# Two loads moved forward and one group of operands split in the front of a convolution and token-mixing kernel

## The chip, the cores and the metric

The kernel runs on one core of a Trainium2 chip. The metric is the device time of one execution in microseconds (us), median over several runs. A ratio is the mean time of the fast runs of one kernel over that of the kernel before in the same rounds, so it is not quite the ratio of the medians that are quoted beside it. The kernel before was timed anew with each group of experiments, since each group ran on another chip (its medians there: 1449.39, 1450.40 and 1449.05 us).

## The reference, cut to what matters

```python
# x: 8 x 4224 x 192 (batch, tokens, channels); 8 heads of 24 channels; 7 taps
w = softmax(weight)                                  # 8 x 7
x = causal 7-tap convolution of x along the tokens, taps w by head
theta = x @ w_theta                                  # 192 x 192
zr, zi = x * cos(theta), x * sin(theta)
y = einsum('ts,bsd->btd', w_tok_r, zr) + einsum('ts,bsd->btd', w_tok_i, zi)   # 4224 x 4224 weights
u = x + y
out = u + maximum(u @ w_ch, 0)
```

## The kernel before

The 4224 tokens are 33 chunks of 128. For each chunk the kernel convolves (`conv`, two halves), transposes the result (`transpose`), multiplies by w_theta (`theta`, two halves), takes sine and cosine on ScalarE, and forms products and sums on VectorE. These become the moving operands of the large product. The weights of that product are loaded in **steps**, turned and combined on VectorE (`w_tasks`: the names "11", "21", "22", "12" are turned blocks, S1 to S4 sums of them), and used by the matmuls of line 443. In the **front**, the first 105 us or so, both kinds of work have to start together: chunks 0 to 10 are made while the first steps already run on those that are ready.

```python
    def banks(name, dtype=F32):              # PSUM buffer of conv, theta and transposes: two of them
        return mmpool.tile([P, 2, PC if dtype == F32 else 2 * PC], dtype, name=name, tag="mm")
    ...
        def w_tasks(self):                   # operands of a step, with their place in the step before
            ...
            return [
                (0.25, lambda: self.turn("11")), (1.2, lambda: self.turn("21")),
                (2.05, lambda: self.wsum("S3")), (2.2, lambda: self.turn("22")),
                (3.05, lambda: self.wsum("S1")), (3.3, lambda: self.wsum("S2")),
                (4.2, lambda: self.turn("12")), (5.1, lambda: self.wsum("S4")),
            ]
    ...
    load_chunk(0)
    ...
    load_chunk(1)
    ...
    steps[0].load_rows()
    for m in (1, 2):
        steps[0].load_w(m)                   # GpSimd queue; two buffers st, one per m
    load_chunk(2)                            # GpSimd queue
    for m in (1, 2):
        steps[1].load_w(m)                   # each waits until step 0 has turned that buffer
    for i in range(NW + 2):                  # NW = 11 chunks
        ...                                  # conv(0), theta(0) of i-1, conv(1), theta(1) of i-1
        if i == 1:
            for _, f in steps[0].w_tasks():
                f()
        if i + 3 < NW:
            load_chunk(i + 3)
        between(1)
        if ch:
            ch.transpose()
        if old:
            old.product(Z11)
        between(2)                           # matmuls of the steps, where ready
        if old:
            old.product(Z21)
        between(1)
        ...                                  # sums(0), sums(1)
```

The order of calls is the order on each compute engine.

Of the kernel before, what the change touches and what calls it, by code (L numbers as in the profile page):

```python
# [16 lines left out]
def kernel(  # L17
# [257 lines left out]
    def load_chunk(k):  # L275
        if k < NK and k not in chunks:
            chunks[k] = Chunk(k, before=chunks[k - 1] if k % NW else None)
# [229 lines left out]
    steps = [Step(t) for t in range(NSTEP)]  # L507
# [72 lines left out]
    def idle(n):  # L580
        for _ in range(n):
            pe(nc.tensor.matmul(
                spare[:, 0, 0:BH], lhsT=noise[:, 0:P], rhs=noise, start=True, stop=True
            ))
# [55 lines left out]
    def more(n):  # L640

        for i in range(n):
            if need[0] is None:
                need[0] = next(flow, NK)
            if need[0] > ready[0]:
                return n - i
            need[0] = next(flow, NK)
        return 0

    steps[0].load_rows()  # L650
    for m in (1, 2):
        steps[0].load_w(m)
    load_chunk(2)
    for m in (1, 2):
        steps[1].load_w(m)
    for i in range(NW + 2):
        ch = chunks.get(i) if i < NW else None
        old = chunks[i - 1] if 0 < i <= NW else None

        def between(n):  # L660
            left = more(n)
            if 0 < i < 3:
                idle(min(left, 2))

        if ch:
            ch.conv(0)
        between(2)
        if old:
            old.theta(0)
        between(1)  # L670
        if ch:
            ch.conv(1)
        if i == 0:
            idle(4)
        ready[0] = i - 2
        between(2)
        if old:
            old.theta(1)
        if i == 1:
            for _, f in steps[0].w_tasks():  # L680
                f()
        if i + 3 < NW:
            load_chunk(i + 3)
        between(1)
        if ch:
            ch.transpose()
        if old:
            old.product(Z11)
        between(2)
        if old:  # L690
            old.product(Z21)
        between(1)
        if old:
            old.sums(0)
        between(1)
        if old:
            old.sums(1)
        between(1)
# [37 lines left out]
```

## Time and profile before

| | before |
|---|---|
| time, median of 3 runs | 1449.51 us (1448.77 to 1449.61) |
| span of the profiled run | 1446.4 us |
| TensorE busy | 1416.3 us, 98% |
| TensorE's wait for x of chunk 3 | 0.88 us, at 26.8 to 27.7 us |

The page's rows of granted TensorE clock and of DMA, in 40 slices of the span (36 us each), are these:

```profile
PEclk9999999999999999999999999999999999999999
DMA  9986756465699998998899989999999999998893
```

In the first three slices, the front, the transfer engines are 80 to 90% busy or more, so the order of transfers counts there. The clock row reads 9 (90% or more) throughout, and hides stretches of a few microseconds at half clock. The lines that the argument rests on are in the prediction.

### The profile page before, as it was taken

What the parts mean: (1) busy time and instruction counts of PE and PEld (TensorE: products, weight loads), DVE (VectorE), ACT (ScalarE), POOL (GpSimd) and SP (SyncE); (2) the same over time, 40 slices, a digit from 0 to 9 for tenths busy, and PEclk for the clock granted to TensorE, in tenths of its full rate; (3) what the DMA queues carried; (4) which work ended last, traced back from release to release, by engine and by line L of the source; (5) the groups of instructions that cost most, each with busy time, mean ns of one, the idle gap of its engine ahead of it and who ended that gap; (6) DMA issues with size and microseconds to landing.
All of it is one profiled execution on the core that took longest, in us unless ns stands there. A gap on an engine that the chain in (4) does not pass through costs nothing.

```text
span 1446.4 us, 23748 instructions
## 1 busy us (share of the span) xinstructions
PE 1416.3 (98%) x9809; PEld 887.9 (61%) x9809; DVE 979.2 (68%) x1051; ACT 315.5 (22%) x379; POOL 435.1 (30%) x655
## 2 busy tenths in 40 slices
PE   7899999999999999999999999999999999999997
PEld 5556666666666666666666666666666666666665
DVE  6893555545548777866666657877777667767686
ACT  5861101111134254000000004435210110010133
POOL 7431211111233232432433342233323123213120
PEclk9999999999999999999999999999999999999999
DMA  9986756465699998998899989999999999998893
GB/s 173 227 178 145 146 103 149 90 149 97 137 231 219 214 250 217 228 254 183 213 256 213 242 143 245 228 188 234 279 216 206 209 204 221 204 203 194 166 222 125
DMA packets 272029, 281.99 MB, mean 195 GB/s; under 512 B 106672, under 2 KB 240176, under 8 KB 271920
## 3 DMA queue, kind: packets, MB, share of 16 engines
q0 software_dynamic: 162464, 92.15, 48.4%
q1 hardware_dynamic: 71824, 178.88, 35.1%
q10 hardware_dynamic: 37632, 9.44, 4.1%
q8 instruction: 77, 1.26, 0.3%
q14 instruction: 32, 0.26, 0.1%
HBM read 245.49 MB, written 108.13 MB: 244 GB/s over the span
## 4 chain that ended last, share of the span: by engine, by line
PE 89%; DVE 4%; DMA 3%; POOL 2%; ACT 1%; issue 1%; SPq 0%; DVEq 0%; ACTq 0%; POOLq 0%
PE y L443 82%; PE v L141 5%; PE pc L210 1%; PE tp L165 1%; POOL st L323 1%; DMA xw<-in_x_dram 1%; DVE z L257 1%; DVE wt L336 1%; DVE pv L408 1%; ACT z L246 1%; DVE z L251 0%; DVE pv L476 0%; DVE wt L348 0%; POOL xw L197 0%; DMA xs<-z 0%
## 5 line engine op out<-in xcount | busy, mean ns | idle before, releaser
L443 PE MATMUL y<-z,wt 128*128 128x384 f16 x7656 | 1283.6, 326 | 10.6 <-DVE pv L408 7.5
L443 PEld LDWEIGHTS <-wt 128*128 128x128 f16 x7656 | 740.8, 98 | 488.6 <-issue 10.6
L408 DVE TENSOR_TENSOR pv<-y,pv 128x768 f32<-128x768 f32 x324 | 308.9, 954 | 323.6 <-PE y L443 282.8
L336 DVE STREAM_TRANSPOSE wt<-st 128x1408 f16<-128x1408 f16 (+7 forms) x224 | 327.8, 1465 | 48.5 <-PE y L443 39.0
L323 POOL DMA_DIRECT2D st<-in_moe_w_tok_r_dram x232 | 132.5, 578 | 466.1 <-DVE wt L336 461.0
L323 POOL DMA_DIRECT2D st<-in_moe_w_tok_i_dram x232 | 132.7, 578 | 404.4 <-DVE wt L336 388.9
L348 DVE TENSOR_TENSOR wt<-wt 128x1408 f16<-128x1408 f16 (+7 forms) x216 | 176.7, 818 | 40.8 <-PE y L443 38.4
L151 ACT ACTIVATE z<-pc 128x768 f16<-128x768 f32 x65 | 53.2, 819 | 387.2 <-PE pc L210 386.9
L151 ACT ACTIVATE ub<-pv 128x768 f16<-128x768 f32 x63 | 50.2, 835 | 333.0 <-DVE pv L408 310.4
L406 ACT ACTIVATE pv<-y 128x768 f32<-128x768 f32 x66 | 54.0, 819 | 282.0 <-PE y L443 282.0
L141 PEld LDWEIGHTS <-uT 128*128 128x128 f16 x1056 | 91.0, 98 | 25.8 <-issue 7.9
L386 POOL TENSOR_TENSOR pv<-pv,xr 128x1536 f32<-128x1536 f32 x24 | 74.5, 3105 | 68.6 <-DVE pv L476 22.1
L197 POOL DMA_DIRECT2D xw<-in_x_dram x132 | 76.4, 585 | 31.0 <-DMA xw<-xw 8.7
L476 DVE SCALAR_TENSOR_TENSOR pv<-v,pv 128x768 f32<-128x768 f32 x66 | 62.9, 954 | 27.5 <-PE v L141 27.1
L257 DVE TENSOR_TENSOR z<-z 128x768 f16<-128x768 f16 x132 | 73.4, 556 | 3.6
L151 ACT ACTIVATE uT<-tp 128x1536 f16<-128x1536 f16 (+1 forms) x48 | 58.2, 1215 | 74.4 <-PE tp L165 74.4
L246 ACT ACTIVATE z<-v,half_pi 128x768 f16<-128x768 f32 x66 | 59.8, 907 | 41.2 <-PE v L141 40.8
L251 DVE TENSOR_TENSOR z<-z 128x1536 f16<-128x1536 f16 x66 | 60.0, 947 | 7.5 <-ACT z L246 7.5
L141 PE MATMUL v<-wth,uT 128*128 128x192 f16 x528 | 55.0, 248 | 4.4 <-ACT z L246 3.0
L141 PE MATMUL v<-wch,uT 128*128 128x192 f16 x528 | 54.2, 246 | 2.1 <-DVE pv L476 1.2
L246 ACT ACTIVATE z<-v 128x768 f16<-128x768 f32 x66 | 53.4, 809 | 0.0
L210 PE MATMUL pc<-xw,bands 96*64 96x192 f16 x528 | 35.8, 258 | 2.6 <-ACT bands L625 1.1
(44 smaller groups left out, 142.4 us busy)
## 6 DMA issues: line engine op xcount, KB each, us to landing
part<-pv SPq DMA_DIRECT2D x79, 768.0 KB, 4.3
pv<-part SPq DMA_DIRECT2D x79, 768.0 KB, 6.1
out_dram<-pv SPq DMA_DIRECT2D x66, 384.0 KB, 4.3
st<-in_moe_w_tok_r_dram POOLq DMA_DIRECT2D x136, 176.0 KB, 5.5
st<-in_moe_w_tok_i_dram POOLq DMA_DIRECT2D x136, 176.0 KB, 5.1
xs<-z SPq DMA_DIRECT2D x132, 96.0 KB, 4.5
xw<-in_x_dram POOLq DMA_DIRECT2D x121, 96.0 KB, 6.1
xr<-xs SPq DMA_DIRECT2D x24, 384.0 KB, 3.7
```

The costliest lines, as they stand in the source:

```text
L141: pe(nc.tensor.matmul(v[:, k, b * D : (b + 1) * D], lhsT=tT[:, 3 * k + b + i, :], rhs=w[:, 2 * b + i, :], start=(i == 0), stop=(i == 1),))
L151: act(nc.scalar.activation(out=out, in_=in_, func=AT.Copy))
L197: nc.gpsimd.dma_start(out=self.xw[lo : lo + n, h, :, :], in_=x[:, t0 : t0 + n, :].rearrange("b s d -> s b d"),)
L246: act(nc.scalar.activation(**args))
L257: dve(nc.vector.tensor_tensor(out=z[:, o, :], in0=z[:, a, :], in1=z[:, b, :], op=ALU.subtract))
L323: pool(nc.gpsimd.dma_start(out=st[a * Q : (a + 1) * Q, 0:nb, :, 0:n] .rearrange("i r bt s -> i (r bt) s"), in_=w[self.tbs[0] * P : (self.t ...
L336: dve(nc.vector.transpose(self.w[name][:, 0 : self.n, :, :], self.st[int(name[1])][:, int(name[0]) - 1, :, 0 : self.n * Q] .rearrange("p b ...
L348: dve(nc.vector.tensor_tensor(out=self.w[name][:, 0 : self.n, :, :], in0=self.w[a][:, 0 : self.n, :, :], in1=self.w[b][:, 0 : self.n, :, : ...
L386: ins = pool(nc.gpsimd.tensor_tensor(out=self.pv[i], in0=self.pv[i], in1=self.xr[i], op=ALU.add))
L408: dve(nc.vector.tensor_tensor(out=o, in0=yv, in1=o, op=ALU.add))
L443: pe(nc.tensor.matmul(y[cn][:, q, 0:BH], lhsT=self.w[wn][:, c, :, :].rearrange("p bt i -> p (bt i)"), rhs=chunks[k].z[:, zn, q * BH : (q + ...
L476: dve(nc.vector.scalar_tensor_tensor(out=ub, in0=channel_mix(self.uT[i][:, 6 * g : 6 * g + 6, :], wch), scalar=0.0, in1=ub, op0=ALU.max, o ...
```

## The change

Intent: bring x of chunk 3 before TensorE asks for it, by loading it ahead of the weights of step 1. So that chunk 2 and chunk 3 can come early, the second weight load of step 0 goes later, and the operands made from it ("22", S1, S2, "12", S4) are made later too.

```diff
     steps[0].load_rows()
-    for m in (1, 2):
-        steps[0].load_w(m)
+    steps[0].load_w(1)
     load_chunk(2)
+    steps[0].load_w(2)
+    load_chunk(3)
     for m in (1, 2):
         steps[1].load_w(m)
@@
         if i == 1:
-            for _, f in steps[0].w_tasks():
-                f()
+            for at, f in steps[0].w_tasks():
+                if at < 2.2:
+                    f()
@@
         if old:
             old.product(Z11)
         between(2)
+        if i == 1:
+            for at, f in steps[0].w_tasks():
+                if at >= 2.2:
+                    f()
         if old:
             old.product(Z21)
```

## The prediction

> **What bounds the kernel now.** I read the page first. One line of it settles the scale:
>
> ```profile
> PE 1416.3 (98%) x9809; PEld 887.9 (61%) x9809; DVE 979.2 (68%) x1051; ACT 315.5 (22%) x379; POOL 435.1 (30%) x655
> ```
>
> PE is busy for 1416.3 of the 1446.4 us of the span, so all its idle time is 30.1 us, and the change touches only the first 105 us or so: after that the tables by stretch of time show PE full (90.00 busy of 90.00 us from 110 to 200, 200.00 of 200.00 from 200 to 400). Two per cent of 1449.5 us is 29 us, as much as all of PE's idle time, so the question is only about a microsecond or two in the front. There I read the timeline of 12 to 42 us, one engine at a time. TensorE, where the front's loop reaches chunk 3 (chunks count from 0):
>
> ```profile
> 25.39 0.98 PE L582 MATMUL y<-noise 128*128 128x384 f16 x5
> 26.58 0.24 PE L210 MATMUL pc<-xw,bands 96*64 96x192 f16 x1 [0.22 <-ACT z L246]
> 27.70 0.52 PE L210 MATMUL pc<-xw,bands 96*64 96x192 f16 x7 [0.88 <-DMA xw<-in_x_dram]
> 28.15 0.83 PE L141 MATMUL v<-wth,uT 128*128 128x192 f16 x8
> ```
>
> The first of 8 convolution matmuls of chunk 3 goes at 26.58, the other seven wait for x until 27.70. This 0.88 us is the wait that the change is after. Where x of chunk 3 stood in the queue is seen on GpSimd:
>
> ```profile
> 12.36 2.29 POOL L197 DMA_DIRECT2D xw<-in_x_dram x4
> 16.41 2.29 POOL L323 DMA_DIRECT2D st<-in_moe_w_tok_r_dram x4 [1.77 <-DVE wt L336]
> 18.68 2.29 POOL L323 DMA_DIRECT2D st<-in_moe_w_tok_i_dram x4
> 20.96 4.57 POOL L197 DMA_DIRECT2D xw<-in_x_dram x8
> 25.97 2.55 POOL L197 DMA_DIRECT2D xw<-in_x_dram x4 [0.44 <-DMA xw<-in_x_dram]
> ```
>
> Chunk 2 is at 12.36; chunk 3 is the first half of the 8 at 20.96, behind both weight loads of step 1, the first of which waited 1.77 us for a buffer that VectorE had yet to empty. Issued from 20.96 to 23.2 and landing 4.7 to 5.0 us later, its last part comes at about 27.6. VectorE over the same time:
>
> ```profile
> 15.35 0.76 DVE L336 STREAM_TRANSPOSE wt<-st 128x256 f16<-128x256 f16 x2
> 16.15 0.29 DVE L348 TENSOR_TENSOR wt<-wt 128x256 f16<-128x256 f16 x1
> 16.36 0.44 DVE L336 STREAM_TRANSPOSE wt<-st 128x256 f16<-128x256 f16 x1
> 16.83 0.62 DVE L348 TENSOR_TENSOR wt<-wt 128x256 f16<-128x256 f16 x2
> 17.36 0.44 DVE L336 STREAM_TRANSPOSE wt<-st 128x256 f16<-128x256 f16 x1
> 17.84 0.29 DVE L348 TENSOR_TENSOR wt<-wt 128x256 f16<-128x256 f16 x1
> 19.71 0.96 DVE L149 COPY uT<-tp 128x1536 f16<-128x1536 f16 x1 [1.58 <-PE tp L165]
> ...
> 25.59 0.96 DVE L149 COPY uT<-tp 128x1536 f16<-128x1536 f16 x1 [0.20 <-PE tp L165]
> 26.46 1.82 DVE L251 TENSOR_TENSOR z<-z 128x1536 f16<-128x1536 f16 x2
> 28.32 2.34 DVE L257 TENSOR_TENSOR z<-z 128x768 f16<-128x768 f16 x4
> 30.57 0.70 DVE L336 STREAM_TRANSPOSE wt<-st 128x512 f16<-128x512 f16 x1
> 32.85 0.96 DVE L251 TENSOR_TENSOR z<-z 128x1536 f16<-128x1536 f16 x1 [1.57 <-ACT z L246]
> ```
>
> The first six rows are the operands of step 0. After them VectorE idles 1.58 us for the transposes of chunk 1. From 19.71 to 31.27 it then has one pause, of 0.20 us, and idles 1.57 us before the first product of chunk 2. So between 19.7 and 31.3 us VectorE is as tight as TensorE.
>
> **What the Trainium skill says.** "TensorE: Matmul & The Clock Gate", the table at its head, has VectorE, ScalarE and GpSimdE working off their queues in strict order. The trace agrees: no operand of step 1 passes another on VectorE, and chunk 3 did not pass the load that waited at 16.41. "DMA: Bandwidth & Descriptors", section "Anatomy of one DMA", says that a semaphore wait happens on the issuing sequencer before dispatch; the 1.77 us on GpSimd is such a wait. The same page's table "Specifications" gives 512 B as the least transfer for full rate; of the 21468 packets of the first 60 us 19577 are under 512 B and the mean rate is 194 GB/s, so transfers there queue up, and order matters. The TensorE page, part 1, has a clock that falls to half after a window of about 3.4 us with little work. Granted clock by microsecond: 0.94, 0.50, 0.50, 0.50, 0.86 from 38 to 43 us, so one such window, and I return to it as a rival.
>
> **The change part by part.** No instruction is added or removed; the order changes on two engines.
>
> Part one, the loads. GpSimd spends 2.29 us per group of four. Chunk 2 goes from 12.36 to 10.08, which gains nothing: its convolution at 20.53 follows the noise matmuls without a pause, 5 us after its x. The second weight load of step 0 goes from 10.08 to 12.36, chunk 3 from 20.96 to 14.65. Chunk 3 lands by 14.65 + 2.29 + some 4 = 21, well before 26.6. Its wait of 0.88 us on TensorE goes.
>
> The first load of step 1 starts at 14.65 + 2.29 = 16.94 in place of 16.41, its buffer being free at about the same time. The second load of step 1 needs the buffer that transposes "22" and "12" empty, and part two moves these.
>
> Part two, the operands. "11", "21" and the first difference stay at 15.35 to 16.44. "22", two sums, "12" and the last difference, 17.84 + 0.29 - 16.36 = 1.77 us, move behind the first product of chunk 0. VectorE then idles from 16.44 to 19.71, because the copy at 19.71 waits for TensorE all the same: the 1.77 us come out of idle time and go into the stretch that had none. The first product ends near 21.5; the five run to 23.3; the second product and sums of chunk 0, at 22.43 + 2.34 = 24.77 before, end at 26.5; the transpose of step 1 ends at 27.1; the copy of chunk 2 starts at 25.59 + 1.77 - 0.20 = 27.16 and ends at 28.12.
>
> That copy feeds the theta matmuls of chunk 2, which come next on TensorE after the convolution. Before they began at 28.15, held back by x. Now x holds nothing back, the convolution ends at 27.1, and they begin at about 28.15 to 28.2, held back by the copy. The 0.88 us removed is put back by VectorE, almost to the tenth. ScalarE's sines of chunk 2 started at 29.02 behind those matmuls and stay there.
>
> Further on: products and sums of chunk 1 end 1.57 us later, at 30.66 + 1.57 = 32.2, the transpose at 32.8, and the product of chunk 2 was at 32.85 waiting for ScalarE. The delay of 1.57 fits into the idle 1.57. Sum: -0.88 from x, +0.9 from the copy, 0.0 to +0.1 from what the idle time can't swallow: about zero, and TensorE beyond 33 us as before.
>
> The loads behind are late, but none is needed soon. Step 1's second load goes at 23.3 in place of 18.68, and at 4 us lands near 29.5; transpose "22" of step 1 came at 34.06. Chunk 4 follows from 25.6 to 27.9, at up to 6.7 us lands by 34.6; its convolution was at 36.72. Chunk 5 lands by some 38, needed at 45.10.
>
> **The rivals.** First, the wait is won in full. It speaks for it that TensorE's wait is named in the trace and ScalarE idled 1.90 us beside it. That would need the copy of chunk 2 early, and VectorE has no gap there. It would make 1449.5 - 0.9 = 1448.6 us. Second, VectorE becomes the bound: if the copy or the products slip more than the slack of 1.57, or chunk 4 arrives after 36.7 because its queue started late, TensorE loses 0.5 to 1.5 us: 1450 to 1451. Third, the half clock from 38.9 to 42.3 us goes or moves. TensorE was continuously busy in it, and at half rate lost about half of 3.4, so 1.7 us. What precedes it are stretches with TensorE half idle (0.08 busy of 35 to 36, 0.69, 0.68, 0.55). A small shift could keep the clock up: 1447.8; or add a second slow window, about 1451. As my sum leaves those stretches as they were, I take the slow window to stay, with one chance in four that it doesn't.
>
> **Range and chances.** Before: 1449.51. The sum is zero; the first and third rival together are somewhat likelier than the second, so I take 0.3 off: 1449.2 us. The runs of before spread over 0.84 us, so their noise is some 0.4 each way; a won wait and a vanished slow window give the low end, 1447.4, a late VectorE the high end, 1450.8. As all idle time together only just makes up the 2 per cent, within 2 per cent has 0.985, faster 0.01, slower 0.005.
>
> **What would show it.** Right: no wait for x before chunk 3's convolution; the copy of chunk 2 near 27.2 and theta matmuls of chunk 2 waiting for it until 28.1 to 28.2; an idle stretch of over 3 us on VectorE before 19.7; the product of chunk 2 near 32.85; GpSimd waiting from about 19.2 to 23.3 for a buffer of step 1. Wrong: theta matmuls of chunk 2 near 27.2 (then the first rival), VectorE's product of chunk 2 past 33.3 or a wait for x of chunk 4 (the second), or granted clock at 1.00 from 38 to 43 us (the third).

## The result, and the profile after

| | before | changed |
|---|---|---|
| median of 4 runs each | 1449.14 us (1448.48 to 1449.61) | 1449.58 us (1445.97 to 1451.64) |
| ratio, 95% interval | | 1.0001 (0.998 to 1.0022) |
| span of the profiled run | 1446.4 us | 1449.8 us |

The time is the same. The profile of the changed kernel, in the same stretch and the same columns (start, length, engine, line, operation, count, wait and what ended it), VectorE first:

```profile
14.28 0.76 DVE L336 STREAM_TRANSPOSE wt<-st 128x256 f16<-128x256 f16 x2
15.07 0.29 DVE L348 TENSOR_TENSOR wt<-wt 128x256 f16<-128x256 f16 x1
19.29 0.96 DVE L149 COPY uT<-tp 128x1536 f16<-128x1536 f16 x1 [3.92 <-PE tp L165]
20.16 0.95 DVE L251 TENSOR_TENSOR z<-z 128x1536 f16<-128x1536 f16 x1
21.02 0.44 DVE L336 STREAM_TRANSPOSE wt<-st 128x256 f16<-128x256 f16 x1
...
26.58 0.92 DVE L149 COPY uT<-tp 128x1536 f16<-128x1536 f16 x1
...
32.25 0.96 DVE L251 TENSOR_TENSOR z<-z 128x1536 f16<-128x1536 f16 x1
```

The five operands begin at 21.02, behind the first product; the idle time before the copy of chunk 1 has grown from 1.58 to 3.92 us; and from there to the product of chunk 2 at 32.25 no line shows a wait at all. TensorE:

```profile
25.99 0.59 PE L210 MATMUL pc<-xw,bands 96*64 96x192 f16 x8
27.56 0.83 PE L141 MATMUL v<-wth,uT 128*128 128x192 f16 x8 [0.98 <-DVE uT L149]
```

All eight convolution matmuls of chunk 3 go together, so the wait for x is gone. In its place theta waits 0.98 us for VectorE's copy. GpSimd:

```profile
19.75 0.58 POOL L323 DMA_DIRECT2D st<-in_moe_w_tok_r_dram  x1 [0.26 <-DMA st<-in_moe_w_tok_i_dram]
22.77 2.28 POOL L323 DMA_DIRECT2D st<-in_moe_w_tok_i_dram  x4 [2.44 <-DVE wt L336]
```

The second load of step 1 waits for the late transposes and goes at 22.77; before it went at 18.68.

The two profiled spans differ by 3.4 us the other way. The change does not account for that, as e1 below shows. Both kernels stop at the end of the front for the same 2.46 us, for an addition on VectorE; the changed kernel gets there 0.8 us earlier:

```profile
104.61 7.65 PE L443 MATMUL y<-z,wt 128*128 128x384 f16 x46 [2.46 <-DVE pv L408]
...
103.82 8.36 PE L443 MATMUL y<-z,wt 128*128 128x384 f16 x40 [2.46 <-DVE pv L408]
```

The first line is of the kernel before, the second of the changed one. In the changed one the clock then fell to half: fewer matmuls (40 against 46) fill more time. In the table by microsecond (TensorE's busy time and count come second, the granted clock is the third number from the end), one line of each kernel, before first:

```profile
106.00:107.00 1.00, 1.00 (x8) 0.60 (x7) 1.00 (x2) 0.00 (x0) 0.87 (x2) 1.00 0.09 8
...
106.00:107.00 1.00, 1.00 (x5) 0.48 (x4) 0.54 (x1) 0.00 (x0) 1.00 (x2) 0.50 0.27 23
```

Five matmuls in a microsecond in place of eight. The record of the changed kernel has three half-clock stretches in its first 110 us (8.7 to 15.5, 36.0 to 39.4, 104.2 to 107.6), that of before has one (38.9 to 42.3). A caution on such records: that of before begins only at 14.98 us, and the views count what is missing as 1.00. Yet the twelve transposes of chunk 0 took 1.49 us at 12.95 and those of chunk 1 0.83 us at 18.84, so it began at half speed too. Later, at 635 us, the changed kernel waits 1.30 us for another addition on VectorE where the kernel before has no wait. Whether these belong to the change is the first question for the experiments.

### The profile page after: what moved, and what is told of

It is laid out like the page before. It is cut to its first block, busy times and chain, and to the rows that moved or that the text cites. A ratio compares the mean times of both kernels' runs of the same rounds, so it can differ in the third digit from the quotient of the medians.

```text
span 1449.8 us, 23748 instructions
## 1 busy us (share of the span) xinstructions
PE 1418.0 (98%) x9809; PEld 887.4 (61%) x9809; DVE 976.5 (67%) x1051; ACT 315.2 (22%) x379; POOL 434.2 (30%) x655
## 4 chain that ended last, share of the span: by engine, by line
PE 86%; DVE 5%; DMA 4%; ACT 2%; issue 2%; POOL 1%; SPq 0%; DVEq 0%; ACTq 0%; POOLq 0%
PE y L443 78%; PE v L141 5%; DMA st<-in_moe_w_tok_i_dram 2%; PE pc L210 1%; PE tp L165 1%; DVE pv L408 1%; ACT z L246 1%; DVE z L257 1%; DVE z L251 1%; DVE wt L336 1%; DMA xw<-in_x_dram 1%; DVE wt L348 1%; ACT pv L406 1%; ACT uT L151 0%; DMA part<-pv 0%
```

## The experiments

Eleven kernels ran, all with correct results. The starts of four instructions serve as milestones, and since the start of the front itself wanders (below), intervals between them say more than times: the copy of chunk 1 on VectorE, the first theta of chunk 2 on TensorE, the first product of chunk 2 and the first addition of a y on VectorE.

### e1: the changed kernel again

No edit.

> The changed kernel once more, unaltered. The four runs on record spread from 1446.0 to 1451.6 us, those of before from 1448.5 to 1449.6. My theory: the change itself moves the front by only -0.2 us (from the copy of chunk 1 to the first theta of chunk 2 8.44 us before, 8.27 after), and the spread comes from how many windows of about 3.4 us with half TensorE clock fall into a run: each costs up to 1.7 us. Then the mean ratio is 1.000 within 0.001, the long runs have the lower mean clock, and the profile again shows 8.2 to 8.3 us over that stretch. Rival: the change makes slow windows more frequent; then this kernel is slower than before by 1 us or more in the median and its mean clock lower than that of the runs of before.

Measured: median 1449.71 us (1445.95 to 1453.25, 6 runs), before 1449.39 (1446.60 to 1450.69, 11 runs), ratio 1.0004 (0.999 to 1.0019). The profiled run has a span of 1444.1 us, 5.7 us less than the first profile **of the same program**. From the copy of chunk 1 to the first theta of chunk 2 it shows 26.55 - 18.28 = 8.27 us again. The 5.7 us build up like this: 1.0 us at the first addition (36.85 and 35.84), 3.2 us at 107 (from 12.5 to 110 us the new profile has no half clock), 4.2 us at 599, and 5.9 us at 640 (no wait at 635); from 644 us on it stays at 5.7. So stretches of half clock and waits at single additions come and go between executions of one program, and a spread of several microseconds belongs to it; the kernel before, with 11 runs, spread over 4.1 us as well. Of the expected link with the mean clock little is seen: the longest run, 1453.25, lists 0.997, and 1450.69 of before lists 0.999. The mean ratio is as my theory had it, and so is the interval in the front; the rival, more slow stretches by the change, has no support.

The records also show when the 2.46 us wait is followed by half clock. In each of them the half-clock stretches, but for one that the end of the program cuts, last 3.41 us or twice that, and they begin whole multiples of 3.41 us apart, so every execution has its own row of marks, 3.41 us from one to the next. Eight profiles have this wait: before, changed, and e1 to e6. In three of them (changed, e3, e5) the whole wait lies between two marks, TensorE is busy for 28% of that stretch, and half clock follows. In the other five a mark cuts the wait in two, TensorE is busy for 50 to 63% of the emptier stretch, and no half clock follows. So where the marks happen to lie decides whether this wait costs 1.7 us more (an estimate: half of 3.41).

### e2 and e3: each half of the change alone

e2 takes the new order of loads and leaves the operands in one part; e3 splits the operands and leaves the loads.

```diff
# e2, against the kernel before
-    for m in (1, 2):
-        steps[0].load_w(m)
+    steps[0].load_w(1)
     load_chunk(2)
+    steps[0].load_w(2)
+    load_chunk(3)
```

```diff
# e3, against the changed kernel
-    steps[0].load_w(1)
+    for m in (1, 2):
+        steps[0].load_w(m)
     load_chunk(2)
-    steps[0].load_w(2)
-    load_chunk(3)
```

> The loads in the new order, the operands of step 0 in one part as before. In the changed kernel the last part of the second weight load of step 0 was issued at 14.45 and took 5.0 us, so it is there at about 19.5. Theory: the five operands wait for it until 19.5, end near 21.3, and the copy of chunk 1, at 19.3 to 19.7 otherwise, starts at about 21.2: all behind it 1.5 to 2 us later, so 1 to 2 us slower than the changed kernel. Rival: that load is no hindrance, the copy of chunk 1 stays near 19.7, the first theta of chunk 2 comes 7.4 us after it in place of 8.3 to 8.4, and the kernel is 1 us faster.

> The operands in two parts, the loads as before. Theory: x of chunk 3 and the late copy of chunk 2 end together, so TensorE waits for x as before (0.9 us) and the copy hides behind it: from the copy of chunk 1 to the first theta of chunk 2 8.4 to 8.7 us, the time within 0.5 us of before. If the delays added, it would be 9.3 us and the kernel 1 us slower.

Measured for e2: 1450.70 us (1448.27 to 1452.09), ratio 1.0010 (0.9998 to 1.0022). VectorE:

```profile
21.03 0.45 DVE L336 STREAM_TRANSPOSE wt<-st 128x256 f16<-128x256 f16 x1 [4.59 <-DMA st<-in_moe_w_tok_r_dram]
```

"22" waited 4.59 us for its weights, until 21.03, and the copy of chunk 1 came at 22.73 in place of 19.71. (The view names `w_tok_r`, whose later load takes the same semaphore. "22" is made from `w_tok_i`, whose last part landed at 20.91.) The mechanism is as expected; that it costs about 1 us in the time is in keeping with the interval but not proved by it.

Measured for e3: 1454.76 us (1453.73 to 1456.38), ratio 1.0039 (1.0026 to 1.0052): **5.4 us slower**, where I had expected nothing. TensorE and GpSimd:

```profile
30.66 0.24 PE L210 MATMUL pc<-xw,bands 96*64 96x192 f16 x1 [4.29 <-DMA xw<-in_x_dram]
31.60 0.85 PE L210 MATMUL pc<-xw,bands 96*64 96x192 f16 x7 [0.70 <-DMA xw<-in_x_dram]
...
23.20 2.29 POOL L323 DMA_DIRECT2D st<-in_moe_w_tok_i_dram  x4 [4.50 <-DVE wt L336]
25.47 4.56 POOL L197 DMA_DIRECT2D xw<-in_x_dram  x8
```

I had looked only at VectorE. The late transposes empty the weight buffer late, the second load of step 1 waits 4.50 us for it at the head of GpSimd's queue, and x of chunk 3 stands behind that load. My own prediction had this wait for the changed kernel, where chunk 3 is ahead of it; I forgot it where chunk 3 is behind. At the first addition e3 is 4.9 us behind the kernel before (42.30 and 37.44), so most of the loss arises in the front. So neither half is worth anything alone: these loads need the split, and the split needs them.

### e4: x behind both weight loads, operands in one part

```diff
# against before
     for m in (1, 2):
         steps[0].load_w(m)
     load_chunk(2)
+    load_chunk(3)
     for m in (1, 2):
         steps[1].load_w(m)
```

> Both weight loads of step 0 first, then x of chunks 2 and 3, then the weights of step 1; operands in one part as before. Theory: the wait for x goes and VectorE's copy of chunk 2 stays where it was, 5.9 us after that of chunk 1, so the first theta of chunk 2 comes about 7.4 us after the copy of chunk 1 (8.44 before, 8.27 changed) and the first product of chunk 2 12.1 us after it (13.14 and 12.96): 0.9 to 1.0 us faster than both, if the gain isn't eaten by the 2.46 us wait at 101 to 104 us, which ends with VectorE. Rival: the front's pace is set by ScalarE and the y buffers, or by VectorE at the later wait: then theta comes early but the time stays within 0.3 us of before.

Measured: 1449.32 us (1447.46 to 1452.30), ratio 1.0003 (0.9991 to 1.0015). VectorE's copy of chunk 2 was early as I wanted (25.85, 6.13 us after that of chunk 1), x was there, and still theta began only 8.20 us after the copy of chunk 1, not 7.4. TensorE and ScalarE:

```profile
26.43 0.59 PE L210 MATMUL pc<-xw,bands 96*64 96x192 f16 x8
27.92 0.82 PE L141 MATMUL v<-wth,uT 128*128 128x192 f16 x8 [0.90 <-ACT z L151]
...
27.05 0.81 ACT L151 ACTIVATE z<-pc 128x768 f16<-128x768 f32 x1 [0.68 <-PE pc L210]
```

Theta waits for ScalarE to clear the convolution of chunk 3. It doesn't read that result, so the wait should be for its buffer. A listing of the PSUM buffers in the built programs shows it: convolutions, theta and transposes of the whole kernel take 250 buffers, the two in turn without exception in the kernel before, but in e4 **and in the changed kernel** the convolution of chunk 3 and the theta after it got the same one. Nothing in the source says so; the build chose it after the loads were moved.

### e5 and e6: the two buffers strictly in turn

```diff
-        tc.tile_pool(name="mmps", bufs=2, space=bass.MemoryType.PSUM)
+        tc.tile_pool(name="mmps", bufs=1, space=bass.MemoryType.PSUM)
...
+        turn_of[0] = 1 - turn_of[0]
         return mmpool.tile([P, 2, PC if dtype == F32 else 2 * PC], dtype,
-                           name=name, tag="mm")
+                           name=name, tag=f"mm{turn_of[0]}")
```

e5 is e4 with this, e6 the changed kernel with this.

> e4 with the two PSUM buffers of convolution, theta and transposes taken strictly in turn, as they are in the kernel before. In e4 the first theta matmul of chunk 2 waited 0.90 us for ScalarE, because the build gave the convolution of chunk 3 and that theta the same buffer. Theory: with the buffers in turn that wait goes, the first theta of chunk 2 comes 7.3 us after the copy of chunk 1 (8.20 in e4, 8.44 before), the first product of chunk 2 about 12.0 us after it (12.88 in e4, 13.14 before), and the lead of about 1.0 us over before lasts at least to 100 us. In the time 1 us is at the edge of what the spread of runs lets one see. Rival: ScalarE or VectorE holds theta back in some other way, then it stays at 8.2.

> The changed kernel with the two PSUM buffers strictly in turn. In it the shared buffer was free at 27.42 and VectorE's copy of chunk 2 ended at 27.50, theta began at 27.56. Theory: VectorE's copy is what holds theta back, so nothing changes: first theta of chunk 2 8.2 to 8.3 us after the copy of chunk 1, first product of chunk 2 12.9 to 13.0, time as the changed kernel within 0.7 us. Rival: the shared buffer was the cause; then theta comes earlier than 8.1.

Measured for e5: 1449.02 us (1448.01 to 1453.10), before 1450.40 (1448.73 to 1456.75, 9 runs), ratio 0.9990 (0.997 to 1.0011). TensorE, with lines 2 later than above:

```profile
26.45 0.59 PE L212 MATMUL pc<-xw,bands 96*64 96x192 f16 x8
26.98 0.83 PE L143 MATMUL v<-wth,uT 128*128 128x192 f16 x8
```

Theta follows the convolution at once, 26.98 - 19.75 = 7.23 us after the copy of chunk 1, and the product of chunk 2 comes at 11.92 us after it. So the 0.90 us of e4 was the buffer. The time shows no difference that its interval could tell from nothing.

Measured for e6: 1449.20 us (1447.00 to 1450.52), ratio 0.9987 (0.9965 to 1.0008); theta at 27.72 - 19.45 = 8.27 us, as without. In the changed kernel the shared buffer therefore cost nothing: VectorE's copy holds theta back, as the prediction had it. In the first profile the buffer was free at 27.42, when ScalarE ended the line below, and the copy (26.58 + 0.92) ended at 27.50:

```profile
26.61 0.81 ACT L151 ACTIVATE z<-pc 128x768 f16<-128x768 f32 x1 [0.68 <-PE pc L210]
```

### e7 and e9: the long wait at the end of the front

The 2.46 us at 102 to 104 us are an addition on VectorE behind products and sums of chunk 10, which no matmul needs before step 5. e7 is the kernel before with these moved into step 4; e9 is the same program again, in the rounds of e10 and e11.

```diff
-        if old:
+        if old and old.k < NW - 1:
             old.product(Z11)             # likewise product(Z21), sums(0), sums(1)
# among the events of a step:
+        if t == base[-1] - 1:            # step 4
+            late = chunks[NW - 1]
+            found.append((1.3, lambda: late.product(Z11)))
+            found.append((2.3, lambda: late.product(Z21)))
+            found.append((3.4, lambda: late.sums(0)))
+            found.append((4.4, lambda: late.sums(1)))
```

> The kernel before, with the two products and the four sums of the last of the front's chunks (10), needed only in step 5, moved from the end of the front into step 4. In all profiles TensorE waits 2.46 us at 102 to 104 us for one addition on VectorE that stands behind them in its queue; they take 1.78 + 2.34 = 4.1 us. Theory: this wait goes, wholly or to under 0.5 us, and 2 to 2.5 us are gained to the end, more where a half-clock window follows the wait: ratio 0.9985 or less. Rival: the wait moves into step 4 or 5, whose operands VectorE makes at that time; then the ratio is 1.000.

> e7 once more, as the quiet twin of the kernel before: its five runs lay within 0.8 us, those of before within 8. Theory: again 1445.4 to 1446.3, and the profile shows no wait of TensorE at 100 to 105 us. Rival: the narrow spread was chance; then it spreads over 3 us or more.

Measured: e7 1445.83 us (1445.44 to 1446.22), before 1450.40, ratio 0.9964 (0.9946 to 0.9982); e9 1446.23 us (1444.72 to 1448.59), before 1449.05 (1447.42 to 1450.63), ratio 0.9980 (0.9967 to 0.9992). Both intervals lie below 1. TensorE in e7 has no wait from 92.91 us to beyond 130:

```profile
92.91 37.38 PE L443 MATMUL y<-z,wt 128*128 128x384 f16 x229
```

The means of the same rounds differ by 5.3 and by 2.7 us. The wait itself is 2.46; in e7's rounds one run of before took 1456.75 us and pulls the mean. The narrow spread of e7 was chance, as e9 shows with 3.9 us.

These two profiles are also two more of the **old order of loads**, and they showed me what one profile could not. e7's front started earlier (copy of chunk 1 at 18.31, before 19.71), yet x of chunk 3 came at the same time, and TensorE waited twice as long:

```profile
27.82 0.52 PE L210 MATMUL pc<-xw,bands 96*64 96x192 f16 x7 [1.83 <-DMA xw<-in_x_dram]
...
19.68 1.15 POOL L323 DMA_DIRECT2D st<-in_moe_w_tok_i_dram  x2 [1.25 <-DMA xw<-in_x_dram]
```

The second line, of GpSimd, tells why the loads didn't start earlier too. With the buffers free earlier, a weight load of step 1 next waits 1.25 us for an earlier transfer to land (the loads of this queue take eight semaphores in turn, so one waits for the eighth before it), and chunk 3 goes at 20.81 where it had gone at 20.96. With the early start x of chunk 2 was late in the old order too: its last part landed at 19.89, and its convolution in e7 waited 0.57 us for it.

The wandering of the start goes with the clock records. In the four profiles whose clock rises to full at 12.4 to 12.5 us (e1, e7, e10, e11) the copy of chunk 1 comes at 18.2 to 18.3, in the two where it rises at 15.5 (changed, e9) at 19.3. Both orders of loads are found with either start.

The profiles with either order, and e5, in us:

| kernel | copy of chunk 1 | theta of chunk 2 | product of chunk 2 | first addition | from copy to addition |
|---|---|---|---|---|---|
| old order: before | 19.71 | 28.15 | 32.85 | 37.44 | 17.73 |
| e7 | 18.31 | 28.27 | 33.45 | 38.05 | 19.74 |
| e9 | 19.32 | 28.85 | 34.09 | 38.68 | 19.36 |
| changed | 19.29 | 27.56 | 32.25 | 36.85 | 17.56 |
| e1 | 18.28 | 26.55 | 31.25 | 35.84 | 17.56 |
| e6 | 19.45 | 27.72 | 32.42 | 37.02 | 17.57 |
| e10 (below) | 18.29 | 26.57 | 31.27 | 35.87 | 17.58 |
| e5 | 19.75 | 26.98 | 31.67 | 36.27 | 16.52 |

In the old order theta comes at 28.2 to 28.9 whenever the front starts: it follows the transfers. In the changed order it comes 8.27 us after the copy whenever that is: it follows VectorE. With an early start, at 18.3, the difference is 28.27 - 26.55 = 1.7 us; with the start of the first profile it is 0.2. The order of e5 isn't free of the transfers either: e11 (below), with the same order and a start at 18.22, has theta at 26.03, 7.81 us after the copy, because VectorE waits 1.14 us at 24.42 for weights of step 1. In e7 and e9 the old order's longer wait was followed by a half clock besides, for 3.4 us from 29.2 to 29.6 on, which is part of their 19.4 to 19.7.

### e8, e10, e11: is there a version that beats both

e8 is e5 with e7's deferral, and a small memset that stands before the late addition moved from VectorE to GpSimd; e10 is the changed kernel with the deferral; e11 is e8 without moving the memset.

```diff
# e8 only
-    dve(nc.vector.memset(wch[:, 1:3, :], 0.0))
+    pool(nc.gpsimd.memset(wch[:, 1:3, :], 0.0))
```

> e5 and e7 together, and the small memset that stands in front of the late addition on VectorE moved to GpSimd. Theory: the gains add, 1.0 + 2.3 us and up to 0.2: 1446 us against 1449.4, ratio 0.9977. Rival: one of the two is eaten by the same wait; then about 1447 us.

> The changed kernel with the same deferral of the last chunk's products and sums, as the quiet twin of the changed kernel. Theory: the change is worth 0.1 to 0.3 us in the front and nothing after, so the median is within 0.5 us of the quiet twin of before. Rival: the long wait near 102 us had hidden a real gain or loss of the change; then the twins differ by 0.8 us or more.

> e5 and e7 together, the small memset left on VectorE. In e8 VectorE waited 5.56 us near 110 us for weights whose loads had let two small loads in between, and the 1.2 us won in the front were gone at 124 us. Theory: without that reordering the front's gain comes on top: 0.8 to 1.2 us faster than the quiet twin of before, some 1444.8. Rival: VectorE's operands for step 5, which now include the last chunk's, set the pace at 105 to 125 us whatever the front does: then within 0.4 us of the quiet twin.

Measured: e8 1445.65 us (1445.26 to 1446.59), ratio 0.9964 (0.9946 to 0.9982), so no better than e7. Its first addition came 1.2 us before e7's, at 36.89, and at 118 to 124 us it was 1.0 to 1.7 us behind:

```profile
114.66 1.65 DVE L338 STREAM_TRANSPOSE wt<-st 128x1408 f16<-128x1408 f16 x1 [5.56 <-DMA st<-in_moe_w_tok_r_dram]
```

VectorE waited 5.56 us for weights. On GpSimd two small loads had come between the four weight loads of `w_tok_i`, at 101.61, and the last of the four landed at 114.53 (the view again names the later load on the same semaphore). In e11, where they don't, it landed at 108.47, and there is no such wait. That the small loads are the cause is argued from the order, not tested by itself.

e10: 1445.52 us (1443.48 to 1447.00), ratio 0.9973 (0.996 to 0.9985). e11: 1445.00 us (1443.96 to 1446.72), ratio 0.9970 (0.9957 to 0.9984). Means of the five runs: e9 1446.5, e10 1445.5, e11 1445.3. By the medians e10 is 0.71 us faster than e9, more than the 0.5 of its theory and less than the 0.8 of the rival. The twins of before and changed differ by 1.0 us in the means, in the direction of the table above, but with spreads of 3.5 to 3.9 us five runs each can't tell that from nothing. What the times do show is that the versions with the deferral are faster than the kernel before, by 2.7 to 5.3 us in the means, and so faster than the changed kernel, whose ratio is 1.000; which of them is best they don't show. The profiles go both ways on whether a lead of the front lasts: e10's lead over e9 was 3.8 us at 60 us and still 4.2 at 1000, while e11's lead over e7, 1.8 us at 404, was lost by 641, with a wait of 1.92 us for one addition at 630.6.

## Why the prediction was right

The predicted time was 1449.2 us within 1447.4 to 1450.8, and the measured median is 1449.58. The chances had 0.985 on "within 2 per cent". That the median came so close is in part luck: two of the four runs lie outside the range, at 1445.97 and 1451.64, because the range reckoned with some 0.4 us of noise each way.

- **x of chunk 3 no longer waits, and VectorE's copy takes the wait's place.** Right, in the trace of the changed kernel: 0.98 us for the copy where 0.88 for x had been. e6 shows that the shared PSUM buffer was not the cause, and e5 that theta comes 1.0 us earlier where the copy is not late.
- **The copy of chunk 2 near 27.2, theta at 28.1 to 28.2, product near 32.85.** Measured 26.58, 27.56 and 32.25, with a start 0.42 us earlier. Taken from the copy of chunk 1, theta was predicted at 8.4 to 8.5 us and came at 8.27; the product at 13.1 and came at 12.96.
- **VectorE's 1.57 us of slack take up the delay.** Right: the product of chunk 2 shows no wait, so the slack was used up to the last tenth. The fixed distance of 17.57 us from the copy of chunk 1 to the first addition, in all four profiles of the changed order, fits this: VectorE has no pause between the copies of chunks 1 and 2, and theta waits for the second.
- **Loads behind come late and nobody needs them.** Right: the second load of step 1 went at 22.77 (23.3 predicted), and no later wait for x or for these weights appears in the front of the changed kernel.
- **The step that was too narrow: "the 0.88 us removed is put back by VectorE, almost to the tenth", and from it a sum of zero.** It takes the arrival of x relative to the rest from one execution. The profiles of e7 and e9 show the same order of loads with waits of 1.83 and 1.69 us, because x arrives when the transfers allow while the rest of the front starts when it will. So the change is worth 0.2 us in the front I had read and up to 1.7 us in others. The first additions come on average at 38.06 us in three profiles of the old order and at 36.40 in four of the new, of which 0.29 is the earlier start and some 0.3 the half clock in e7 and e9 (9.8 us from theta to addition, 9.3 elsewhere). The times of 4 to 11 runs can't show it: the ratios 1.0001, 1.0004 and 0.9987 (e6) all include 1. Whether a gain of about 1 us reaches the end stays open.
- **The third rival, a half-clock stretch that moves or is added.** It happened, in both of its forms, and it is larger than the change. I gave it one chance in four. In the first profile of the changed kernel the window near 39 us stayed (36.0 to 39.4) and one was added at 104.2; in e1, the same program, neither came. With the cold start the two record about 13.7 and 3.4 us of half clock in the first 110 us. That the centre held because such stretches fall on both kernels is argued, not shown.
- **Slips in the working.** The low end of the range doesn't follow from its terms: 1449.5 - 0.9 - 1.7 is 1446.9, not 1447.4. The convolution of chunk 2 did not come 5 us after its x: the last part landed at 18.88, 1.65 us before. So moving chunk 2 forward "gains nothing" only with the late start of that profile; in e7, with the early start, that convolution waited 0.57 us for x, in e1 and e10, where chunk 2 is forward, it did not.
- **What I had not seen at all:** the shared PSUM buffer, which by luck was free 0.08 us before the copy ended.

## What to carry to other kernels

When one wait is removed, ask what ends next at the same place: here the transfer, VectorE's copy and a PSUM buffer ended within a microsecond of each other, and taking away one or two of the three gained 0.2 us at most in the profiles with the start of the first one. Read an interval from several executions before you put a size on it, above all where one side of it is paced by transfers and the other by compute, and where stretches of half clock and waits at single additions make two profiles of one program differ by 5.7 us. And look for the longest wait of the critical engine first: work that nobody needed yet stood in front of one addition, and moving it was worth more than all reordering of loads.

## What the Trainium skill lacked or had wrong

- "TensorE: Matmul & The Clock Gate", part 1 and the closing section "Why this matters for your kernels", has the clock fall to half after an idle window and asks for no idle gaps above some 3 us. Here it fell after shorter gaps: in the changed kernel at 104.2 us after one wait of 2.46 us, and in the kernel before at 38.9 us after 3.4 us in which TensorE was about half busy and no single wait was over 1.3 us. Part 1 also knows a kernel that fell back through frequent short idles, but the page doesn't say how much work is enough. In these thirteen profiles, cut from 16 us on at the marks that e1 describes, every stretch of 3.41 us at full clock in which TensorE was busy for less than 45% was followed by half clock (25 of them), and none of those with more than 53%; in between both occur.
- The same page calls the cold start run-variable and less than 1% of a kernel. Both hold here: the copy of chunk 1, where nothing else delayed it, came between 18.2 and 20.4 us, along with the clock's rise (see e7), and this 2.2 us is 0.15% of 1449. But it lacks the warning that this is larger than many a change worth testing.
- "DMA: Bandwidth & Descriptors", section "Anatomy of one DMA", fits one load on GpSimd's queue as 2.0 us plus size over 436 GB/s, 2.2 us for the 96 KB of x. With the queue full, as in this front, those of chunks 2 to 5 landed 3.8 to 5.0 us after issue in the changed kernel, and those issued from 42 to 47 us up to 9.6 us after. The page has no figure for a load among many in flight.
- "Perfetto Trace Analysis", section "Matmuls", advises to rotate independent matmul groups through different PSUM banks. It doesn't say to check that the build does so: here two groups in a row got one buffer, at 0.90 us in e4.
